# The last block's product with W34 goes between the first nine products of the second mixture; token factors move to other attention slices, and those of batch 3 to GpSimd one by one

## The chip, the core and the metric

The kernel runs on one core of a Trainium2 chip, in one launch. The metric is device time in microseconds (us) of that launch; lower is better. The core has TensorE (PE, with its weight loads as PEld), VectorE (DVE), ScalarE (ACT), GpSimd (POOL) and SyncE (SP), which here only issues DMAs. Each engine takes its instructions in the order in which the program has them, and an instruction that waits holds up those behind it.

## The reference

Three layers follow each other, all in float32: a linear attention with a decaying state, a gated product with two more matrices behind it, and eight experts whose outputs are summed with weights from a Sinkhorn iteration.

```python
# attention, batch 4, 8 heads, 768 steps, head size 48
for t in range(S):
    cur = np.einsum('bhd,bhe->bhde', u[None] * kt, vt)
    y[:, :, t] = np.einsum('bhd,bhde->bhe', rt, state + cur)
    state = wt[:, :, :, None] * state + np.einsum('bhd,bhe->bhde', kt, vt)
# first mixture, 3072 tokens, 384 -> 1024 -> 384
h = (x @ w1) * (x @ w2) @ w3
x2 = h @ w_out
# second mixture, 8 experts, 384 -> 1024 -> 384
logits = x2 @ w_gate;  P = np.exp(logits - logits.max())
for _ in range(8):
    P /= P.sum(1, keepdims=True) + 1e-09
    P /= P.sum(0, keepdims=True) + 1e-09
    P *= N / E
for e in range(E):
    out += P[:, e:e + 1] * (np.maximum(x2 @ w1[e], 0.0) @ w2[e])
```

## The kernel before

Every float32 product is made of three passes on TensorE: both operands are split into a high and a low part, and high·high, high·low and low·high are added in PSUM. ACT makes the high part (a copy that rounds), DVE or POOL the low part (a subtraction).

**First half of the program.** A loop over *slices* `s` carries the attention and the first mixture side by side. Attention has 24 units of 128 steps (6 for each of the 4 batches); a unit takes four slices: in the first, `stage_a0` starts the factors of the next unit; in the second, `stage_b` issues the score products `sc` and the transposes `trn`, and DVE masks the scores (`copy_predicated`, L329); in the third, `stage_c1` uses them (`yt<-ec,nat_v`, `up`) and DVE updates the state (`Sn`); in the fourth, `stage_c2` finishes `yt` and ACT copies it to `xraw`. The factors of the next unit are queued in `aux` and taken two for each slice; on DVE these are the two scans `Ft` and `Gt` in the first slice, `Kt` in the second, `Rt` in the third, the reduction `cc` in the fourth.

The first mixture works on blocks of 384 tokens (8 blocks, two for a batch). Each block has 8 slices `moe_a`/`moe_b` (products `pa`, `pb`, their elementwise product `gs`, its parts `gh` and `gl`), and then 4 slices `moe_x2` (18 matmuls `po` each) that multiply by W34 = w3·w_out, which was made early. ACT copies `po` into `x2[batch]`, nine slots of 128x256 for each batch. The dictionary `slices` says which slice does what. Block 7, the last, has its `moe_a`/`moe_b` in slices 99 to 106 and its `moe_x2` in 107 to 110, behind the end of attention (slice 95).

**Second half.** The second mixture multiplies tokens by the experts' w1 with a scheme that needs 15 block products instead of 18: `ORDER` is their order, `WA` and `XC` say which sums of weight blocks and of token blocks are the two factors of each. The token factors of a batch (15, each a high and a low part of 128x256) are made once, stored in DRAM (`xd`), and loaded again for each of the 16 pairs of weight rows. They come in four groups of four, four, four and three. The work is a loop over *phases* `n` = 0 to 63 (batch `n % 4`); a phase issues 15 products `zp` of six matmuls (128x256 moving), and behind each the function `after(r)` runs: it loads or makes what is due, and it takes `YN[r]` units of `y`, the second product of the phase before (24 units of three matmuls `yp`, 128x384 moving). `later(d, f)` puts a function `d` products later. Results of `zp` go through ACT copies (`cp`, L877) and DVE additions (L870, L873) into `ct`, then ACT makes `hh` (L862) and DVE `hl` (L867). Several products add on top of a bank that has to be read first: product 9 follows product 8 in bank b, with a copy on ACT between them.

**Who makes token factors.** `pre_x` makes one factor in a slice of the first half: sums on DVE (L707) at the end of a slice, the high part on ACT (L711) at the end of the next, the low part on DVE (L714) and the store to `xd` (L717) at the end of the one behind it. `PRE` gives one factor to each slice from the slice behind a batch's last `moe_x2`, for batches 0 and 1 all fifteen, for batch 2 the first eight. Scratch is `x2[3]`, the tile of batch 3, which is empty until block 6 writes it. The rest, groups 2 and 3 of batch 2 and all of batch 3, is made in phases 1 and 2 on POOL by `sp_x`, a group at a time, three products between its sums and its high part.

Of the kernel before, what the change touches and what calls it, by code (L numbers as in the profile page):

```python
# [32 lines left out]
def tile_rwkv_moe_sinkhorn_moe(  # L33
# [278 lines left out]
    def stage_b(n):  # L312
        d = st[n]
        Rt, Kt = d["R"], d["K"]
        sc = [ps.tile([P, NP, DP], F32, tag=f"sc{h}", name=f"sc{h}") for h in range(2)]
# [6 lines left out]
        pn = ps.tile([P, NP, P], F32, tag="yt0", name="trn")  # L322
# [11 lines left out]
    def stage_c1(n):  # L334
# [3 lines left out]
        up = [ps.tile([P, NP, DP], F32, tag=f"sc{c}", name=f"up{c}") for c in range(2)]  # L338
        yp = [ps.tile([P, NP, DP], F32, tag=f"yt{c}", name=f"yt{c}") for c in range(2)]
# [306 lines left out]
    def sp_w1(i, g, eng, tmp_=None):  # L646
# [91 lines left out]
    for blk in range(NB):  # L738
# [3 lines left out]
        for q in range(X2S):  # L742
# [4 lines left out]
    late = [logs.pop(x) for x in sorted(logs) if x >= NSL]  # L747
    stage_a0(0)
# [446 lines left out]
```

## Time and profile before

| | |
|---|---|
| median of 3 runs | 2028.53 us (2026.86 to 2029.04) |
| the profiled execution | 2026.48 us, of which the span from first to last instruction is 2024.7 us |
| PE busy | 1947.3 us, 96% of the span |
| DVE, ACT, POOL busy | 1429.1, 680.8, 676.7 us |
| mean granted TensorE clock | 0.99 of full speed |

The span is that of the profile and holds idle time at its start and end as well; the time of a run is a little longer than its span. A busy engine is one that has an instruction under way. In rows of the timeline, the bracket at the end is the idle time of that engine just before, and the instruction that ended it as far as the trace shows; "issue" means that it shows none.

### The profile page before, as it was taken

Reading aid. Unit: us, or ns where it says so; the run is one execution under the profiler, and the core shown is the slowest. Engines: PE = TensorE matmul, PEld = TensorE weight load, DVE = VectorE, ACT = ScalarE, POOL = GpSimd, SP = SyncE. Lnnn points to the kernel's source line nnn. Section 1 sums busy time; section 2 is a strip of 40 time slices with the busy share of each in tenths; the row PEclk is TensorE's granted clock in tenths of the full one; section 3 lists DMA queues with packets and bytes.
Section 4 is the critical chain, followed back from the end, with each engine's and each line's share of the span. In section 5 each row is a group of like instructions: output and inputs, shape, how many; then the busy total and the mean of one; then the engine's idle time right before and its main releaser. Section 6 shows DMA issues by size and latency. Waiting matters only on the chain.

```text
span 2024.7 us, 37936 instructions
## 1 busy us (share of the span) xinstructions
PE 1947.3 (96%) x15499; PEld 1882.2 (93%) x15499; DVE 1429.1 (71%) x2285; ACT 680.8 (34%) x1292; POOL 676.7 (33%) x865
## 2 busy tenths in 40 slices
PE   5779999999899999999999999999999999999999
PEld 3469898999789999999999999999999999999999
DVE  7865787864788777777666777666776666776666
ACT  4533333333333323323333333323333333333221
POOL 4676565652473122222223131322222232313200
PEclk9889999999999999999999999999999999999999
DMA  7632343423455555555455555555455555555453
GB/s 259 228 106 92 120 137 121 137 67 136 146 201 175 174 189 186 198 181 194 170 201 169 195 186 195 182 188 194 174 200 180 182 182 195 172 198 180 163 202 120
DMA packets 86125, 347.99 MB, mean 172 GB/s; under 512 B 10112, under 2 KB 30144, under 8 KB 60352
## 3 DMA queue, kind: packets, MB, share of 16 engines
q1 hardware_dynamic: 85952, 345.57, 49.5%
q8 instruction: 122, 2.00, 0.4%
q14 instruction: 51, 0.42, 0.1%
HBM read 323.90 MB, written 20.45 MB: 170 GB/s over the span
## 4 chain that ended last, share of the span: by engine, by line
PE 88%; DVE 6%; issue 2%; DMA 2%; ACT 1%; POOL 1%; SPq 1%; DVEq 0%; ACTq 0%; POOLq 0%
PE yp L85 38%; PE zp L85 33%; PE pa L85 5%; PE pb L85 5%; PE po L85 4%; DVE ct L870 1%; PE yt L85 1%; DVE hl L867 1%; PE sc L85 1%; PE trn L85 1%; PE w34ps L85 1%; PE up L85 0%; DMA nat_w<-in_w_dram 0%; DMA raw<-in_moe_w_out_dram 0%; PE pl L85 0%
## 5 line engine op out<-in xcount | busy, mean ns | idle before, releaser
L85 PE MATMUL zp<-xc,w1c 128*128 128x256 f32 x5760 | 844.4, 283 | 16.3 <-ACT ct L877 12.2
L85 PEld LDWEIGHTS zp<-xc,w1c 128*128 128x128 f32 x5760 | 792.6, 189 | 33.7 <-ACT ct L877 14.6
L85 PE MATMUL yp<-w2h,hh 128*128 128x384 f32 x1536 | 517.9, 337 | 0.0
L85 PE MATMUL yp<-w2h,hl 128*128 128x384 f32 x1536 | 517.2, 337 | 0.0
L85 PE MATMUL yp<-w2l,hh 128*128 128x384 f32 x1536 | 516.2, 336 | 0.0
L862 ACT ACTIVATE hh<-ct 128x512 fp32r<-128x512 f32 x384 | 237.7, 632 | 610.6 <-DVE ct L873 331.0
L870 DVE TENSOR_TENSOR ct<-ct,zp 128x512 f32<-128x512 f32 x576 | 381.7, 683 | 55.3 <-PE zp L85 52.8
L626 POOL TENSOR_TENSOR w1c<-w1s,w1c 128x512 fp32r<-128x512 f32 (+1 forms) x120 | 132.9, 1107 | 778.3 <-PE zp L85 477.5
L867 DVE SCALAR_TENSOR_TENSOR hl<-ct,hh 128x512 fp32r<-128x512 f32 x384 | 292.5, 775 | 0.0
L85 PEld LDWEIGHTS yp<-w2h,hh 128*128 128x128 f32 x1536 | 291.6, 190 | 0.4 <-issue 0.4
L85 PEld LDWEIGHTS yp<-w2l,hh 128*128 128x128 f32 x1536 | 288.9, 188 | 0.2 <-DVE w2l L674 0.2
L85 PEld LDWEIGHTS yp<-w2h,hl 128*128 128x128 f32 x1536 | 288.7, 188 | 0.0
L877 ACT ACTIVATE ct<-zp 128x512 f32<-128x512 f32 x256 | 152.7, 596 | 398.4 <-PE zp L85 398.4
L1027 DVE SCALAR_TENSOR_TENSOR acc<-yp,Pm,acc 128x384 f32<-128x384 f32 x336 | 205.2, 611 | 58.6 <-PE yp L85 58.5
L873 DVE TENSOR_TENSOR ct<-ct,zp 128x512 f32<-128x512 f32 x128 | 87.9, 687 | 170.7 <-PE zp L85 170.6
L873 DVE TENSOR_TENSOR ct<-zp,ct 128x512 f32<-128x512 f32 x128 | 88.5, 692 | 137.0 <-PE zp L85 133.3
L618 POOL TENSOR_TENSOR w1s<-w1raw 128x128 f32<-128x128 f32 x240 | 124.0, 537 | 9.3
L441 POOL TENSOR_TENSOR gl<-gs,gh 128x384 fp32r<-128x384 f32 x64 | 76.0, 1188 | 134.0 <-ACT gh L440 128.3
L626 POOL TENSOR_TENSOR w1c<-w1raw,w1c 128x128 fp32r<-128x128 f32 (+1 forms) x90 | 50.4, 560 | 207.8 <-ACT w1c L622 207.8
L85 PE MATMUL pa<-xhl,w1h 128*128 128x384 f32 x384 | 106.8, 359 | 2.7 <-ACT xhl L407 1.9
L85 PE MATMUL pb<-xhl,w2h 128*128 128x384 f32 x384 | 98.7, 338 | 1.6 <-ACT w2h L203 1.6
L439 DVE TENSOR_TENSOR gs<-pb,asb 128x384 f32<-128x384 f32 x64 | 35.3, 552 | 79.6 <-PE pb L85 56.2
(136 smaller groups left out, 1976.8 us busy)
## 6 DMA issues: line engine op xcount, KB each, us to landing
xc<-xd SPq DMA_DIRECT2D x188, 1024.0 KB, 4.9
xc<-xd SPq DMA_DIRECT2D x62, 768.0 KB, 4.3
w1raw<-in_e_w_dram SPq DMA_DIRECT2D x32, 384.0 KB, 3.2
w2raw<-in_e_w_dram SPq DMA_DIRECT2D x32, 384.0 KB, 3.2
xd<-x2s SPq DMA_DIRECT2D x38, 256.0 KB, 2.7
raw<-in_moe_w_dram SPq DMA_DIRECT2D x8, 1024.0 KB, 4.9
nat_w<-in_w_dram SPq DMA_DIRECT2D x24, 264.5 KB, 3.2
nat_k<-in_kt_dram SPq DMA_DIRECT2D x24, 256.0 KB, 3.9
```

Of the source, the lines that this page charges most:

```text
L85: nc.tensor.matmul(o, lhsT, rhs, start=start, stop=stop, **kw)
L439: nc.vector.tensor_tensor(gs, pb, asb, op=ALU.mult)
L441: nc.gpsimd.tensor_tensor(gl[:, f, :], gs, gh[:, f, :].bitcast(F32), op=ALU.subtract)
L618: eng.tensor_tensor(tmp_[:, many.index(r), :], at_(a), at_(b), op=ALU.add if sg == 1 else ALU.subtract)
L626: eng.tensor_tensor(lo[:, d0:d1, :], sv, hi[:, d0:d1, :].bitcast(F32), op=ALU.subtract)
L862: nc.scalar.activation(hh, src, AF.Relu)
L867: nc.vector.scalar_tensor_tensor(hl, src, 0.0, hh.bitcast(F32), op0=ALU.max, op1=ALU.subtract)
L870: nc.vector.tensor_tensor(o, a, b_, op=ALU.add)
L873: nc.vector.tensor_tensor(o, a, b_, op=ALU.subtract)
L877: nc.scalar.activation(t, src, AF.Copy)
L1027: nc.vector.scalar_tensor_tensor(dst, yp, Pm[:, tt, e:e + 1], dst, op0=ALU.mult, op1=ALU.add)
```

## The change

- `moe_x2` of block 7 leaves its four slices. Its 72 matmuls go in nine parts of eight into `after(r)` of the first nine products of phase 0. The PSUM banks of the attention get a pool of their own (`psa`), which is closed at slice 95, so that the banks `zp` (pool `psz`) exist before the first mixture is over; the banks `y`, the tiles behind `m2` and the tiles `ct` (now in pool `m`) are arranged to fit (`open2` runs behind the ninth product).
- The first eight units of `y` of phase 0 run at the end of phase 0 (two, two and four of them), the other sixteen in phase 1, one behind most products.
- `pre_x` is placed by `PLACES` and `LASTPLACES`: sums at the end of third and fourth slices of a unit, the high part in the middle of the next slice, the low part at the end of the third slice of the next unit (when the sums were in a third slice: at the end of the fourth slice of the same unit). There are four workspaces in place of three.
- Groups 2 and 3 of batch 2 are made by `pre_group` on DVE in slices 96 to 98. All of batch 3 is made by `pre_x` on POOL, one factor at a time, from product 11 on (counted from the start of phase 0; `XAT`), with four products between sums and high part.
- The weight factors of pair 1's first row (`sp_w1(2)`) go from phase 0 to phase 2, still on POOL, with a lag of five products in place of two.

```diff
+    st_pa = ExitStack()
+    psa = st_pa.enter_context(tc.tile_pool(name="psa", bufs=1, space=PSUM, side="right"))
...
+    def moe_x2(blk, i, parts=X2S):
         gh, gl = g_t[blk]
-        for m in range(i * X2N, (i + 1) * X2N):
+        n_ = KD * NF * 3 // parts
+        for m in range(i * n_, (i + 1) * n_):
...
+            tmp_ = pools["m"].tile([P, 4, P], F32, tag="w1s", bufs=2, name="w1s")
+        t = pools["m2" if k == 2 else "w"].tile([P, 2, n_, P], F32R, tag=f"w1c{k}{g}", name=f"w1c{k}{g}")
...
+    def pre_x(sb, r, work, ws, eng):
+        g = GOF[r]
+        h_ = work[:, 2 * ws:2 * ws + 2, :]
+        hr = h_.bitcast(F32R)
+        ts = sorted(terms(XC[r]), key=lambda t: t[0] == "-")
+        at_ = [x2[sb][:, SLOT[b], :] for _, b in ts]
+        sv = at_[0] if len(ts) == 1 else h_[:, 1, :]
+
+        def sums():
+            for m, (sg, _) in enumerate(ts[1:], 1):
+                eng.tensor_tensor(h_[:, 1, :], at_[0] if m == 1 else h_[:, 1, :], at_[m],
+                                  op=ALU.add if sg == "+" else ALU.subtract)
+
+        def high():
+            nc.scalar.activation(hr[:, 0, :], sv, AF.Copy)
+
+        def low():
+            eng.tensor_tensor(hr[:, 1, :], sv, h_[:, 0, :], op=ALU.subtract)
+            if (sb, g) not in xd:
+                xd[sb, g] = dram.tile([P, 2, len(XP_[g][4]), T], F32, name=f"xd{sb}{g}")
+            nc.sync.dma_start(xd[sb, g][:, :, XP_[g][4][r], :], h_)
+
+        return sums, high, low
...
+    def pre_group(sb, g, tag, tmp_, eng):
+        t = pools["w"].tile([P, 2, len(XP_[g][4]), T], F32R, tag=tag, name="xpre")
...
-    PRE = {}
-    for sb_ in range(NS - 1):
-        s0_ = 8 * UB * (sb_ + 1) + LAG + NF + X2S
-        for m_, r_ in enumerate(ORDER):
-            if s0_ + m_ < 4 * NU - 1:
-                PRE[s0_ + m_] = (sb_, r_, (m_ + 1) % 3)
-    PRED = {(sb_, g_) for sb_ in range(NS) for g_ in range(NGR)
-            if len(WP_[g_][4]) == sum(x[0] == sb_ and GOF[x[1]] == g_ for x in PRE.values())}
...
-        for q in range(X2S):
+        for q in range(X2S if blk < NB - 1 else 0):
...
+    def place(s, task, high, low):
+        event(s, lambda: task[0]())
+        event(high, lambda: task[1]())
+        event(low, lambda: task[2]())
...
+    PLACES = [4 * UB + 1 + d for d in (3, 3, 6, 7, 7, 10, 11, 11, 14, 15, 15, 18, 19, 19, 22)]
+    LASTPLACES = [4 * UB + 1 + d for d in (3, 3, 4, 6, 7, 7, 8, 10)]
+    for sb_ in range(NS - 1):
+        ends = 8 * UB * (sb_ + 1) + LAG + NF + X2S - 4 * UB - 4
+        for m_, (r_, d_) in enumerate(zip(ORDER, LASTPLACES if sb_ == NS - 2 else PLACES)):
+            s_ = ends + d_ - 0
+            low_ = s_ + {3: 3, 2: 1, 0: 2}[s_ % 4]
+            place(s_ + 0.75, lazy(lambda sb_=sb_, r_=r_, m_=m_: pre_x(sb_, r_, x2[NS - 1], m_ % 4, nc.vector)),
+                  s_ + 1.25, low_ + 0.5)
+    for g_ in range(2):
+        place(4 * NU + g_ + 0.75,
+              lazy(lambda g_=g_: pre_group(NS - 2, 2 + g_, f"xc{g_}",
+                                           pools["w"].tile([P, 4, T], F32, tag=f"w1c{g_}0", name="xtmp"), nc.vector)),
+              4 * NU + g_ + 1.25, 4 * NU + g_ + 1.5)
+    for g_ in range(2 * NGR):
+        place(4 * NU + UB + g_ + 0.75,
+              lazy(lambda g_=g_: sp_w1(g_ // NGR, g_ % NGR, nc.vector,
+                                       tx0[0][:, 2 * (g_ % 3):2 * (g_ % 3) + 2, :]
+                                       .rearrange("p a (b c) -> p (a b) c", c=P))),
+              4 * NU + UB + g_ + 1.25, 4 * NU + UB + g_ + 1.5)
+    tx0 = []
...
-        for task in fx:
-            task.pop(0)()
-        while fx and not fx[0]:
-            fx.popleft()
-        if s in PRE:
-            fx.append(list(pre_x(*PRE[s])))
-            fx[-1].pop(0)()
-        if s == 4 * NU + 1:
+            st_pa.close()
+            pools["z"] = ctx.enter_context(tc.tile_pool(name="psz", bufs=1, space=PSUM, side="right",
+                                                        reuse_waits="tile"))
...
+    PO = 9
+    YN1 = dict(zip(ORDER, (1, 1, 1, 1, 1, 1, 1, 1, 1, 1, 2, 1, 1, 1, 99)))
...
+            if n == 0:
+                i_ = ORDER.index(r)
+                if i_ < PO:
+                    moe_x2(NB - 1, i_, PO)
+                if i_ == PO - 1:
+                    open2()
+                if i_ == 11:
+                    y_fill(0)
+                y_units((0, 0, 2, 2, 4)[max(0, i_ - 10)])
+            elif n == 1:
+                y_units(YN1[r])
...
-        if n + 1 < NS and (n + 1, g) not in PRED:
-            spread(0, XLAG, sp_x(n + 1, g, nc.gpsimd))
-        else:
-            ld_x(n + 1, g)
+        ld_x(n + 1, g)
...
+    XAT = (11, 13, 14, 16, 18, 19, 21, 23, 24, 26, 28, 29, 31, 33, 34)
...
+        if n > 1:
             y_fill(n - 1)
         if n < N:
             if n == 0:
-                for i in range(2):
-                    later(8 + 3 * i, lambda i=i: sp_w2(i))
-                for g in range(NGR):
-                    later(3 * g + 1, lambda i=2, g=g: spread(0, 2, sp_w1(i, g, nc.gpsimd)))
+                for m, at_ in enumerate(sorted(ev)):
+                    later(m, *ev[at_])
+                later(8, lambda: sp_w2(0))
+                later(10, lambda: sp_w2(1))
+                for m, r in enumerate(ORDER):
+                    task = lazy(lambda r=r, m=m: pre_x(NS - 1, r, x2[2], m % 4, nc.gpsimd))
+                    d = XAT[m]
+                    later(d, task[0])
+                    later(d + 4, task[1], task[2])
             if 2 * NS <= n < 3 * NS:
                 ex.extend([lambda sb=sb, t=t: rescale(sb, t) for t in range(S // P)])
+            if n == 2:
+                for g in range(NGR):
+                    later(3 * g + 6, lambda g=g: spread(0, 5, sp_w1(2, g, nc.gpsimd)))
```

The order of instructions shows the moves at three places. First TensorE, where block 7's last product `pb` ends; `po` is the product with W34, `zp` the second mixture. Before:

```order
L85 MATMUL pb<-xhl,w2h 128x384 x2
L85 MATMUL pb<-xhl,w2l 128x384
L85 MATMUL po<-gh,w34h 128x384
L85 MATMUL po<-gl,w34h 128x384
L85 MATMUL po<-gh,w34l 128x384
```

With the change:

```order
L85 MATMUL pb<-xhl,w2h 128x384 x2
L85 MATMUL pb<-xhl,w2l 128x384
L85 MATMUL zp<-xc_5692,w1c_5643 128x256 x3
L85 MATMUL zp<-xc_5692,w1c_5797 128x256 x3
L85 MATMUL po<-gh,w34h 128x384
L85 MATMUL po<-gl,w34h 128x384
L85 MATMUL po<-gh,w34l 128x384
```

The first product of the mixture now stands ahead of the 72 matmuls `po`, eight of which follow it; the same alternation goes on up to the ninth product.

Second DVE, in the first two slices of unit 11 (batch 0's factors are being made: rows named `x2s`). Before:

```order
L270 SCALAR_TENSOR_TENSOR Ft<-nat_w_102,d_63 128x528
L439 TENSOR_TENSOR gs<-pb,asb 128x384
L273 SCALAR_TENSOR_TENSOR Gt<-nat_w_102,d_63 128x527
L714 TENSOR_TENSOR x2s<-x2s 128x256
L707 TENSOR_TENSOR x2s<-x2s 128x256 x2
L329 COPY_PREDICATED ec<-mask,sc_2540 128x256
L329 COPY_PREDICATED ec<-mask,sc_2541 128x256
```

With the change:

```order
L272 SCALAR_TENSOR_TENSOR Ft<-nat_w_105,d_63 128x528
L441 TENSOR_TENSOR gs<-pb,asb 128x384
L275 SCALAR_TENSOR_TENSOR Gt<-nat_w_105,d_63 128x527
L331 COPY_PREDICATED ec<-mask,sc_2539 128x256
L331 COPY_PREDICATED ec<-mask,sc_2540 128x256
```

Three operations of token factors no longer stand between the scans and the masking. Where they stand instead is seen best at the end of unit 13, ahead of the scans that are issued in unit 14. Before:

```order
L304 TENSOR_REDUCE cc<-rk 128x8
L714 TENSOR_TENSOR x2s<-x2s 128x256
L270 SCALAR_TENSOR_TENSOR Ft<-nat_w_103,d_63 128x528
L439 TENSOR_TENSOR gs<-pb,asb 128x384
L273 SCALAR_TENSOR_TENSOR Gt<-nat_w_103,d_63 128x527
```

With the change:

```order
L306 TENSOR_REDUCE cc<-rk 128x8
L702 TENSOR_TENSOR x2s<-x2s 128x256
L695 TENSOR_TENSOR x2s<-x2s 128x256 x4
L272 SCALAR_TENSOR_TENSOR Ft<-nat_w_106,d_63 128x528
L441 TENSOR_TENSOR gs<-pb,asb 128x384
L275 SCALAR_TENSOR_TENSOR Gt<-nat_w_106,d_63 128x527
```

One operation of token factors stood ahead of the scan there; now there are five.

Third DVE between the end of attention and block 7's first product, where the low parts `xhl` of block 7's three pieces are made. Before:

```order
L714 TENSOR_TENSOR x2s<-x2s 128x256 x2
L408 TENSOR_TENSOR xhl<-xraw,xhl 128x3x128
L714 TENSOR_TENSOR x2s<-x2s 128x256
L408 TENSOR_TENSOR xhl<-xraw,xhl 128x3x128 x2
L439 TENSOR_TENSOR gs<-pb,asb 128x384
```

With the change, from the second of the three pieces:

```order
L410 TENSOR_TENSOR xhl<-xraw,xhl 128x3x128
L628 TENSOR_TENSOR xpre<-x2s,xpre 128x256
L628 TENSOR_TENSOR xpre<-xtmp,xpre 128x768
L620 TENSOR_TENSOR xtmp<-x2s 128x256
L620 TENSOR_TENSOR xtmp<-xtmp,x2s 128x256
L620 TENSOR_TENSOR xtmp<-x2s 128x256
L620 TENSOR_TENSOR xtmp<-xtmp,x2s 128x256
L620 TENSOR_TENSOR xtmp<-x2s 128x256
L620 TENSOR_TENSOR xtmp<-xtmp,x2s 128x256
L410 TENSOR_TENSOR xhl<-xraw,xhl 128x3x128
L628 TENSOR_TENSOR xpre<-xtmp,xpre 128x768
```

Two low parts of group 2 and six sums of group 3 now stand between the second piece and the third.

## Rows read from the trace of the kernel before

**Rows 1.** The page: busy us (share of the span), instructions of TensorE.

```profile
PE 1947.3 (96%) x15499; PEld 1882.2 (93%) x15499; DVE 1429.1 (71%) x2285; ACT 680.8 (34%) x1292; POOL 676.7 (33%) x865
```

**Rows 2.** Windows: block 7's last product, then phases 0, 1, 2, 3, 4–6, 7.

```profile
core 0: us, PE busy (x) PEld busy (x) DVE busy (x) ACT busy (x) POOL busy (x), PEclk, DMA share, GB/s
490.72:503.20 12.48, 12.48 (x74) 12.48 (x74) 4.26 (x8) 2.75 (x9) 3.37 (x5) 1.00 0.59 236
503.20:519.90 16.70, 12.27 (x91) 11.05 (x91) 8.51 (x13) 7.58 (x16) 8.98 (x13) 1.00 0.54 188
519.90:550.40 30.50, 26.98 (x187) 25.66 (x186) 21.15 (x39) 8.66 (x16) 7.11 (x8) 0.94 0.40 135
550.40:576.90 26.50, 24.43 (x167) 23.52 (x166) 23.99 (x39) 10.35 (x18) 20.88 (x19) 1.00 0.40 151
576.90:605.40 28.50, 25.27 (x169) 24.90 (x168) 25.07 (x44) 9.20 (x16) 20.28 (x27) 0.94 0.54 202
605.40:680.00 74.60, 71.57 (x496) 69.99 (x495) 59.41 (x118) 24.39 (x46) 17.09 (x28) 1.00 0.53 180
680.00:703.20 23.20, 23.20 (x163) 22.99 (x162) 15.56 (x26) 7.17 (x14) 6.61 (x10) 1.00 0.50 171
```

**Rows 3.** Timeline of TensorE in phase 7: start, us, what, count.

```profile
700.25 0.87 PE L85 MATMUL zp<-xc,w1c 128*128 128x256 f32 x6
700.96 0.34 PE L85 MATMUL yp<-w2h,hh 128*128 128x384 f32 x1
```

**Rows 4.** Timeline of TensorE, waits in phases 0, 1 and 3.

```profile
517.68 3.14 PE L85 MATMUL zp<-xc,w1c 128*128 128x256 f32 x24 [1.35 <-DVE ct L870]
...
525.56 0.98 PE L85 MATMUL zp<-xc,w1c 128*128 128x256 f32 x6 [3.52 <-ACT ct L877]
...
582.08 1.65 PE L85 MATMUL zp<-xc,w1c 128*128 128x256 f32 x6 [3.23 <-ACT ct L877]
```

**Rows 5.** Windows of four attention units: 8, 11, 13 and 7.

```profile
186.83:202.67 15.84, 15.84 (x205) 14.89 (x204) 9.71 (x17) 4.74 (x11) 11.82 (x13) 1.00 0.10 28
235.24:255.24 20.00, 17.74 (x206) 16.66 (x205) 17.07 (x25) 6.16 (x16) 12.24 (x12) 0.91 0.23 75
271.85:289.81 17.96, 16.26 (x208) 15.22 (x205) 15.46 (x28) 6.50 (x15) 10.91 (x12) 1.00 0.38 123
...
170.89:186.83 15.94, 15.94 (x208) 15.03 (x205) 8.77 (x18) 5.68 (x12) 10.52 (x11) 1.00 0.27 93
```

**Rows 6.** Timeline, all engines, unit 11: masking and what stands ahead of it.

```profile
237.75 1.84 POOL L267 TENSOR_TENSOR rk<-rk,ub 128x384 f32<-128x384 f32 x1
...
238.70 1.17 DVE L714 TENSOR_TENSOR x2s<-x2s 128x256 fp32r<-128x256 f32 x1
...
239.79 1.67 DVE L707 TENSOR_TENSOR x2s<-x2s 128x256 f32<-128x256 f32 x2
...
241.38 0.77 DVE L329 COPY_PREDICATED ec<-mask,sc 128x256 f32<-128x256 uint32 x2
...
241.91 0.91 PE L85 MATMUL yt<-ec,nat_v 64*64 64x64 f32 x30 [2.26 <-issue]
...
243.28 0.42 DVE L714 TENSOR_TENSOR x2s<-x2s 128x256 fp32r<-128x256 f32 x1
```

**Rows 7.** Timelines of DVE and TensorE, unit 14: scan, masking, product.

```profile
288.63 2.07 DVE L270 TENSOR_TENSOR_SCAN Ft<-nat_w,d 128x528 f32<-128x528 f32 x1
...
292.58 0.76 DVE L329 COPY_PREDICATED ec<-mask,sc 128x256 f32<-128x256 uint32 x2
...
294.16 0.69 PE L85 MATMUL yt<-ec,nat_v 64*64 64x64 f32 x32
```

**Rows 8.** Timelines ahead of block 7: SP's stores, ACT, TensorE.

```profile
457.35 1.26 SPq L717 DMA_DIRECT2D xd<-x2s  x2
...
462.20 0.55 ACT L470 ACTIVATE x2s<-po 128x256 f32<-128x256 f32 x2 [8.68 <-DMA xd<-x2s]
...
464.66 0.44 PE L85 MATMUL pa<-xhl,w1h 128*128 128x384 f32 x1 [0.15 <-DVE xhl L408]
```

**Rows 9.** Groups by line and shape, POOL, 500 to 620 us: busy, mean ns.

```profile
L618 POOL TENSOR_TENSOR tx<-x2s 128x256 f32<-128x256 f32 x15 | 12.5, 844 | 0.4
```

More of the change, by code (lines that the diff above doesn't have):

```diff
@@ L314, in stage_b @@
         Rt, Kt = d["R"], d["K"]
-        sc = [ps.tile([P, NP, DP], F32, tag=f"sc{h}", name=f"sc{h}") for h in range(2)]
+        sc = [psa.tile([P, NP, DP], F32, tag=f"sc{h}", name=f"sc{h}") for h in range(2)]
         for p in range(NP):
@@ L321, in stage_b @@
                        True, True, pos=(64 * h, 64 * c))
-        pn = ps.tile([P, NP, P], F32, tag="yt0", name="trn")
+        pn = psa.tile([P, NP, P], F32, tag="yt0", name="trn")
         for p in range(NP):
@@ L337, in stage_c1 @@
         first = n % UPB == 0
-        up = [ps.tile([P, NP, DP], F32, tag=f"sc{c}", name=f"up{c}") for c in range(2)]
-        yp = [ps.tile([P, NP, DP], F32, tag=f"yt{c}", name=f"yt{c}") for c in range(2)]
+        up = [psa.tile([P, NP, DP], F32, tag=f"sc{c}", name=f"up{c}") for c in range(2)]
+        yp = [psa.tile([P, NP, DP], F32, tag=f"yt{c}", name=f"yt{c}") for c in range(2)]
         d["yp"] = yp
@@ L747, in tile_rwkv_moe_sinkhorn_moe, with event, run, lazy @@
     late = [logs.pop(x) for x in sorted(logs) if x >= NSL]
+    ev = {}
+    def event(at_, f):
+        ev.setdefault(at_, []).append(f)
+    def run(at_):
+        for f in ev.pop(at_, ()):
+            f()
+    def place(s, task, high, low):
+        event(s, lambda: task[0]())
+        event(high, lambda: task[1]())
+        event(low, lambda: task[2]())
+    def lazy(make):
+        box = []
+        def step(i):
+            if not box:
+                box.append(make())
+            box[0][i]()
+        return [lambda i=i: step(i) for i in range(3)]
+    PLACES = [4 * UB + 1 + d for d in (3, 3, 6, 7, 7, 10, 11, 11, 14, 15, 15, 18, 19, 19, 22)]
[19 more added lines that the diff above has]
+    tx0 = []
     stage_a0(0)
@@ L794, in tile_rwkv_moe_sinkhorn_moe @@
                 x2[si] = xp.tile([P, KD * NR, T], F32, tag="xa", bufs=NS, name="x2s")
+        run(s + 0.5)
+        run(s + 0.75)
         if s == 4 * NU - 1:
@@ L842, in z_new @@
     def z_new():
-        return ps2.tile([P, 2, T], F32, tag="z", bufs=4, name="zp")
+        return pools["z"].tile([P, 2, T], F32, tag="z", bufs=4, name="zp")
     def z_prod(bank, n, r, start, stop):
@@ L1008, in unit @@
             if first:
-                yt[b_, h_] = ps2.tile([P, DM], F32, tag="y", bufs=3, name="yp")
+                yt[b_, h_] = pools["y"].tile([P, DM], F32, tag="y", bufs=3, name="yp")
             yp = yt[b_, h_]
@@ L1068, in sk_max2 @@
-        mm(pm, ones[0:1, :], mrow[0:1, 0:1], True, True)
-        nc.vector.tensor_copy(nmx, pm)
-        nc.scalar.activation(Pm.rearrange("p t e -> p (t e)"), L.rearrange("p t e -> p (t e)"), AF.Exp,
-                             bias=nmx, scale=1.0)
+        pm = pools["y"].tile([P, 1], F32, tag="col", name="pmb")
+        mm(pm, so["ones"][0:1, :], so["mrow"][0:1, 0:1], True, True)
+        nc.vector.tensor_copy(so["nmx"], pm)
+        nc.scalar.activation(so["Pm"].rearrange("p t e -> p (t e)"), L.rearrange("p t e -> p (t e)"), AF.Exp,
+                             bias=so["nmx"], scale=1.0)
@@ L1080, in sk_rows2 @@
[L1080 removed]
+        nc.vector.tensor_tensor(so["Pm"], so["Pm"], so["rs"].unsqueeze(2).to_broadcast([P, NTT, E]), op=ALU.mult)
+        nc.vector.tensor_reduce(so["cs"], so["Pm"].rearrange("p t e -> p e t"), axis=AX.X, op=ALU.add)
     def sk_cols():
[L1083 to L1086 removed]
@@ L1087, in sk_cols @@
-        nc.vector.tensor_scalar(cs, cs, float(NT) / float(E), None, op0=ALU.mult)
+        pc = pools["y"].tile([P, E], F32, tag="col", name="pcs")
+        mm(pc, so["ones"], so["cs"], True, True)
+        nc.vector.tensor_scalar(so["cs"], pc, 1e-9, None, op0=ALU.add)
+        nc.vector.reciprocal(so["cs"], so["cs"])
+        nc.vector.tensor_scalar(so["cs"], so["cs"], float(NT) / float(E), None, op0=ALU.mult)
     def sk_cols2():
-        nc.vector.tensor_tensor(Pm, Pm, cs.unsqueeze(1).to_broadcast([P, NTT, E]), op=ALU.mult)
+        nc.vector.tensor_tensor(so["Pm"], so["Pm"], so["cs"].unsqueeze(1).to_broadcast([P, NTT, E]), op=ALU.mult)
```

113 lines of the change are left out of this document (36 added, 77 removed).

## Prediction

> **What bounds the kernel now.** The page comes first: TensorE is busy for 96% of the span [rows 1], and the change neither adds nor removes a matmul, so it can only win or lose idle time of TensorE, or clock. The windows by stage say where such time is. A phase of the second mixture that nothing disturbs is phase 7: 23.20 us for 15 products and 24 units, TensorE busy throughout [rows 2]. A product's start lies 0.71 us ahead of the next instruction's [rows 3], so 15 cost 10.7 us, and a unit costs (23.20 − 10.7)/24 = 0.52 us. The 72 matmuls of block 7's last product took 12.48 us, TensorE busy throughout, or 1.39 us for eight [rows 2]. Against these prices the start of the mixture is slow: phase 0, which has no units, took 16.70 us for 10.7 us of products; phases 1, 2 and 3 took 30.50, 26.50 and 28.50, and phases 4 to 6 together 74.60 in place of 69.6 [rows 2]. That is 6.0 + 7.3 + 3.3 + 5.3 + 5.0 = 26.9 us above phase 7's pace. The waits name the cause: in phase 0 additions on DVE, in phases 1 and 3 the ACT copy `ct` [rows 4].
>
> The windows of the attention units show a second loss. Unit 11 took 20.00 us where unit 8, its like, took 15.84; unit 13 took 17.96 where unit 7 took 15.94 [rows 5]. Units 17 and 19 repeat 11 and 13 in batch 1, so four units lose 2 × (4.16 + 2.02) = 12.4 us. The timeline of unit 11 shows how: three operations of token factors keep DVE from 238.70 to 241.4, the masking comes behind them and TensorE's `yt<-ec,nat_v` stands for 2.26 us [rows 6]. The bracket says "issue", yet the masking ends as the product starts. The rest of the 4.16 us is clock: the window's mean is 0.91 [rows 5], so 9% of 20 us, 1.8 us, is lost to a stretch at 1.2 GHz behind the gap; unit 13, with the smaller loss, shows 1.00.
>
> **Attention part.** The sums, highs and lows are the same operations at other places. In units 11, 13, 17 and 19 nothing of them is left between scans and masking, so 12.4 us can come back. They now stand in third and fourth slices, mostly where DVE is idle, but in unit 13 five of them stand ahead of the scan where one stood. An operation costs 0.42 us undisturbed and 0.84 to 1.17 with POOL at work [rows 6]. The scan of unit 14 began at 288.63; masking ended at 293.34 and the product started at 294.16, so 0.82 us are to spare [rows 7]. Four more operations cost 1.7 to 3.4 us, of which 0.9 to 2.6 us reach TensorE; I take 1.7, nearer the disturbed price, since POOL works in that slice. Batch 1 repeats it: 3.4 us. Unit 11 keeps two operations ahead of its scan as before and gives back nothing more. Net 12.4 − 3.4 = **9.0 us**. Bounds: 12.4 if the five fit, and 12.4 − 5.2 − 2 × 1.8 (two spells of half clock) − 1.4 (a store that is not through when its workspace is written again, 0.7 us twice) = 2.2.
>
> **Ahead of block 7.** Now ACT stands for 8.68 us until a store issued at 457.35 has landed and released `x2[3]`; it goes on at 462.20, 4.85 us after the issue, and the second matmul of `pa`, the first to need DVE's `xhl`, starts at 464.66 [rows 8]. With the change the last store of token factors still stands behind six small DMAs and I leave its landing between 459.7 and 461.9. Behind it come, in order, an ACT copy and the highs of group 2 (1.5 us), two lows on DVE (four times 256 columns, 1.7 us at 0.42), six sums (2.5 to 3 us) and only then the third `xhl` (0.6 us): 6.3 to 6.8 us, so 466.0 to 468.7, a loss of 1.3 to 4.0 us against 464.66. I take **2.4 us**; bounds 0, if the store lands earlier than I think, and 5.8, with 1.8 us of clock.
>
> **Start of the mixture.** Phase 0 now holds block 7's product and eight units. Its first nine products cost 9 × (0.71 + 1.39) = 18.9 us; the 1.39 us of `po` behind each cover the ACT copies that products 2 and 3 wait for. The last six cost 6 × 0.71 + 8 × 0.52 = 8.4 us, and keep the wait for DVE of 1.35 us [rows 4], as nothing stands behind products 10 to 12: 28.6 us. Phase 1 has 16 units, 19.0 us for TensorE alone. DVE's load decides there: it was busy 59.41 us in phases 4 to 6, 19.8 a phase, and 24 to 25 where POOL worked for 20 us [rows 2]. Batch 3's factors are 15 sums and 15 lows; at 0.844 us [rows 9] they are 25 us on POOL, spread over 28 products, some 13 us of it in phase 1. DVE then needs about 22.5 us (two accumulations less), and with 1.5 us of its backlog from phase 0 I take 24.0. Phases 2 and 3 share the rest with `sp_w1(2)` and `sp_w1(3)`; no group of six or more POOL operations now stands ahead of an ACT copy, and I take 25.0 each, with phases 4 to 6 at 74.0. Sum 28.6 + 24.0 + 25.0 + 25.0 + 74.0 = 176.6, against 12.48 + 16.70 + 30.50 + 26.50 + 28.50 + 74.60 = 189.3: **12.7 us** less. Bounds: at TensorE's pace in all phases (27.3 + 20.5 + 23.2 + 23.2 + 72 = 166.2) 23; with phases 1 to 6 as long as now, less 4.2 us of moved units, 4.8.
>
> On POOL and DVE the Trainium skill (page "SBUF — State Buffer", section "Who interferes with whom") speaks against the change: a DVE instruction with two SBUF inputs waits out a POOL instruction that reads SBUF, rather than sharing with it. The low part that took 1.17 us while POOL's 1.84 us operation ran, and 0.42 without it [rows 6], agrees in direction. By that rule all six `hl` of phase 1, which read `ct` and `hh`, could each wait out one POOL operation, which is the first rival below.
>
> Moved at no cost: the loads of groups 2 and 3 of batch 0 still leave when the last `pb` is through, and have eight products and 64 `po`, 17 us, to land; without that cover phase 0 would stand for what is missing. `memset` of the `ones` tile stands behind the last `po` on DVE, with DVE idle there.
>
> **Sum.** 9.0 − 2.4 + 12.7 = 19.3 us. The profiled execution took 2026.48 us, so 2007.2; the median lies 2.05 us above it, so **2009.2** on its scale. 0.2%, 4 us, is about what a measurement tells from no change.
>
> **Rivals.**
> 1. *DVE stays the bound while POOL works.* Single operations block DVE as often as groups did, and phases 1 to 6 keep their lengths: 9.0 − 2.4 + 4.8 = 11.4 us, **2017**. For it: DVE's 24 to 25 us in phases 2 and 3. Against: DVE had less to do in phase 1 and TensorE still waited, for ACT.
> 2. *All cover holds.* The five operations fit and the mixture runs at TensorE's pace: 28 to 35 us, **1994 to 2000**. Against: DVE's 19.8 us in the least disturbed phases.
> 3. *The stalls only move.* Attention gains 2.2, block 7 loses 5.8, the mixture gains 4.8: 1.2 us, **2027**, the change not doing what it says.
> 4. *Slower: ACT hangs on POOL.* Each of the fifteen highs stands on ACT, ahead of the copies `ct` that TensorE needs, and waits for POOL's sums. If each cost the 3.23 us that the group in phase 3 cost [rows 4], 48 us would be lost and the time be **2057**. It decides from 19.3/15 = 1.3 us a factor. Against: four products, some 5 us, lie between sums and high, for at most two sums of 0.84 us.
>
> **How the numbers follow.** Forecast, 2002 to 2015: 0.66. Rival 1, 2015 to 2022: 0.15. Rival 2: 0.10. Rival 3: 0.04. Rival 4: 0.05. A range from 2000 to 2019 leaves out rivals 3 and 4, half of rival 2 and an edge of rival 1. Faster takes the forecast and rivals 1 and 2: 0.91; same, rival 3: 0.04; slower, rival 4: 0.05.
>
> **What would show it.** In the profile after, units 11, 13, 17 and 19 take about 16 us and units 14 and 20 some 17.5; the first matmuls of block 7's `pa` wait 2 to 5 us; phase 0 takes 28 to 29 us with no wait in its first nine products, phase 1 about 24, with DVE busy for over 90% of it. The forecast is wrong if units 14 and 20 stand longer than 3 us, if a load of token factors ends a wait of TensorE in phase 0 or 3, or if ACT's copies in phases 1 and 2 stand behind highs that wait for POOL.

## The result and the profile after

The changed kernel takes 2007.18 us (median of 5 runs, 2005.56 to 2009.96), the kernel before 2028.53 us in the same session (5 runs, 2026.33 to 2031.01): a ratio of 0.9896, 95% interval 0.9882 to 0.9911, or 21.4 us less. The forecast was 2009.2 us and a gain of 19.3.

The profiled execution of the changed kernel is the slowest of its five (2009.96 us, span 2008.0), that of before was among the quickest of its own, so the two traces show 16.5 us of the 21.4 (16.7 in their spans). Term by term, from the traces:

| stage | before | after | gain | forecast |
|---|---|---|---|---|
| to the start of unit 6 | 154.3 | 154.3 | 0 | 0 |
| units 11, 13, 17, 19 | 75.91 | 63.56 | 12.4 | 12.4 |
| units 14 and 20 | 31.68 | 37.66 | −6.0 | −3.4 |
| unit 23 and block 7 to the end of `pb` | 49.48 | 50.42 | −0.9 | −2.4 |
| from there to phase 7 | 189.3 | 181.4 | 7.8 | 12.7 |
| phase 7 to the end | 1344.7 | 1341.3 | 3.4 | 0 |

The page of the changed kernel, engine row; TensorE has the same instructions and is busy 7.4 us less [rows 1].

```profile
PE 1939.9 (97%) x15499; PEld 1875.6 (93%) x15499; DVE 1416.7 (71%) x2299; ACT 683.8 (34%) x1300; POOL 656.7 (33%) x859
```

Windows of the changed kernel, columns as in [rows 2]: units 11, 14 and 20; then unit 23 with block 7 up to the end of `pb`; phases 0, 1, 2, 3, and 4 to 6; phases 8 to the end.

```profile
235.24:251.09 15.85, 15.85 (x207) 14.90 (x206) 14.31 (x22) 5.58 (x15) 11.87 (x12) 1.00 0.30 94
283.63:303.20 19.57, 17.68 (x205) 16.54 (x204) 15.64 (x25) 5.76 (x14) 10.89 (x12) 0.91 0.24 76
384.16:402.25 18.09, 16.19 (x205) 15.11 (x204) 15.81 (x25) 5.76 (x14) 10.90 (x12) 1.00 0.26 87
434.82:485.24 50.42, 48.38 (x405) 46.88 (x404) 32.44 (x74) 21.91 (x52) 11.61 (x11) 1.00 0.38 131
485.24:514.50 29.26, 28.17 (x188) 27.48 (x187) 15.25 (x27) 10.35 (x22) 1.84 (x2) 1.00 0.63 235
514.50:536.77 22.27, 21.60 (x161) 20.13 (x161) 14.15 (x30) 7.72 (x18) 6.82 (x10) 1.00 0.66 202
536.77:562.55 25.78, 24.25 (x167) 23.55 (x167) 21.51 (x40) 10.25 (x20) 18.69 (x25) 1.00 0.77 249
562.55:592.72 30.17, 26.17 (x168) 25.79 (x167) 23.87 (x46) 9.06 (x20) 17.95 (x29) 0.89 0.57 203
592.72:666.67 73.95, 71.17 (x495) 69.60 (x495) 59.24 (x117) 24.22 (x46) 17.09 (x28) 1.00 0.53 182
689.80:2008.01 1318.21, 1314.66 (x9145) 1300.82 (x9144) 920.61 (x1460) 419.03 (x774) 311.37 (x499) 1.00 0.52 184
```

The two of these windows that have no row ahead of the prediction, in the kernel before:

```profile
441.24:490.72 49.48, 48.59 (x405) 46.84 (x405) 26.25 (x59) 18.57 (x47) 11.22 (x11) 1.00 0.31 102
703.24:2024.72 1321.48, 1318.11 (x9145) 1304.82 (x9144) 923.40 (x1460) 419.08 (x773) 312.44 (x499) 1.00 0.53 183
```

Three places of the changed kernel fall short of the forecast or differ from it. First unit 14, timeline of DVE, POOL, ACT and TensorE:

```profile
281.91 1.03 POOL L443 TENSOR_TENSOR gl<-gs,gh 128x384 fp32r<-128x384 f32 x1 [0.20 <-ACT gh L442]
281.98 4.75 DVE L695 TENSOR_TENSOR x2s<-x2s 128x256 f32<-128x256 f32 x4
...
282.90 1.24 POOL L307 TENSOR_TENSOR ec<-eye,cc 128x512 f32<-128x512 f32 x1
...
284.10 1.19 POOL L268 TENSOR_TENSOR rk<-nat_rn,nat_kn 128x384 f32<-128x384 f32 x1
...
285.37 1.08 POOL L269 TENSOR_TENSOR rk<-rk,ub 128x384 f32<-128x384 f32 x1
...
286.65 1.24 DVE L272 TENSOR_TENSOR_SCAN Ft<-nat_w,d 128x528 f32<-128x528 f32 x1
...
288.81 0.58 ACT L328 ACTIVATE kn<-trn 128x512 f32<-128x512 f32 x1
...
289.94 1.30 PE L85 MATMUL yt<-ec,nat_v 64*64 64x64 f32 x30 [1.89 <-ACT asb L428]
```

The four sums take 1.19 us each, since POOL works beside them: each ends 0.28 to 0.29 us after one of the four POOL operations (the sums at 283.23, 284.42, 285.57 and 286.73). The scan starts at 286.65, 3.0 us after the unit; in [rows 7] it started 1.2 us ahead of it (the unit began at 289.81, [rows 5]). ACT's copy `kn` stands in turn behind work that waits for DVE. TensorE stands for 1.89 us; the mean clock of 0.91 in the window above is a stretch at 1.2 GHz behind that gap, 9% of 19.57, or another 1.8 us. Unit 20 has the same gap (1.90) and, in this execution, no such stretch.

Second, ahead of block 7 (timeline, DVE and TensorE): group 2's lows and group 3's six sums, then the third `xhl`, as forecast. The six sums cost 0.4 us each here, where POOL is idle.

```profile
456.19 0.42 DVE L620 TENSOR_TENSOR xtmp<-x2s 128x256 f32<-128x256 f32 x1
...
458.57 0.55 DVE L410 TENSOR_TENSOR xhl<-xraw,xhl 128x384 fp32r<-128x384 f32 x1
...
459.18 0.44 PE L85 MATMUL pa<-xhl,w1h 128*128 128x384 f32 x1 [2.04 <-DVE xhl L410]
```

Third, the start of phase 3. TensorE stands for 4.00 us at 568.48, and this is the chain of waits that led there (start, us, what):

```profile
551.42 4.12 DMA xd<-x2s
...
555.60 0.75 POOL x2s L695
...
557.19 0.42 ACT x2s L699
557.61 0.53 ACT hh L894
...
558.17 0.69 DVE hl L899
...
560.69 0.82 DVE Pm L1126
...
564.67 1.13 DVE rs L1111
...
566.12 0.56 DVE ct L902
...
566.70 0.63 ACT hh L894
567.33 0.61 ACT w1c L624 x2
567.94 0.49 ACT ct L909
...
568.48 1.65 PE zp L85 x6
```

Read from the top: a store of a token factor has to land before POOL may use its workspace again; POOL's two sums follow; ACT's high part of that factor has been standing on ACT for them and lets the copies `hh` behind it through; DVE, which had run dry, starts a queue of 8.5 us in which steps of the Sinkhorn iteration (`Pm`, `rs`) take 2.5; only behind that queue comes the copy `ct` that product 9 needs.

### The profile page after: what moved, and what is told of

Same layout as the page of the kernel before. It is cut to its first block, busy times and chain, and to the rows that moved or that the text cites. A ratio compares the mean times of both kernels' runs of the same rounds, so it can differ in the third digit from the quotient of the medians.

```text
span 2008.0 us, 37981 instructions
## 1 busy us (share of the span) xinstructions
PE 1939.9 (97%) x15499; PEld 1875.6 (93%) x15499; DVE 1416.7 (71%) x2299; ACT 683.8 (34%) x1300; POOL 656.7 (33%) x859
## 4 chain that ended last, share of the span: by engine, by line
PE 88%; DVE 5%; DMA 2%; POOL 2%; ACT 1%; issue 1%; SPq 0%; DVEq 0%; POOLq 0%; ACTq 0%
PE yp L85 38%; PE zp L85 32%; PE pa L85 5%; PE po L85 4%; PE pb L85 4%; PE w34ps L85 1%; PE yt L85 1%; DMA xd<-x2s 1%; DVE ct L902 1%; DVE hl L899 1%; PE sc L85 1%; PE trn L85 1%; PE up L85 1%; DMA raw<-in_moe_w_dram 0%; DMA raw<-in_moe_w_out_dram 0%
```

## Experiments

Two questions were open: which edit brought what, and what made phase 3 slow. For the second there were two theories, both about the wait of 4.00 us at the start of phase 3. **Theory 1:** ACT stands for POOL, as in rival 4, but at one place. **Theory 2:** DVE is late by its own load. All edits are to the changed kernel unless said otherwise. The runs were made in several sessions; the kernel before took 2028.1 to 2029.2 us in each of them.

**Old places of the token factors.**

```diff
-            s_ = ends + d_ - 0
+            s_ = ends + 4 * UB + 4 + m_
...
-                  s_ + 1.25, low_ + 0.5)
+                  s_ + 1.75, s_ + 2.75)
```

> The changed kernel with the old timetable of token factors (one factor a slice in batches 0 to 2, sums at the end of a slice, high part a slice later, low part two slices later); all else as changed. If the attention part is worth what the traces say, units 11, 13, 17 and 19 take 20, 18, 20 and 18 us again, units 14 and 20 go back to 15.84 us, and the kernel is 6 us slower than the changed one (about 2013). The rival, that the new places only shift stores and transfers and the gain lies elsewhere: within 2 us of the changed kernel.

2022.53 us (6 runs), 15 us more than the changed kernel. Windows of units 11 and 14:

```profile
234.95:254.95 20.00, 17.74 (x205) 16.66 (x204) 17.06 (x25) 6.16 (x16) 12.23 (x12) 0.91 0.25 80
289.51:305.35 15.84, 15.84 (x205) 14.89 (x204) 10.87 (x17) 4.62 (x11) 11.90 (x12) 1.00 0.20 66
```

These units, and unit 13 with 17.95, are those of before to 0.01 us, so the places alone make the attention term. The total was missed: in this combination unit 23 and block 7 take 55.2 us in place of 50.4, with two waits of 1.9 and 2.9 us for `xhl`, as batch 2's last factors then stand in the slices where groups 2 and 3 are made on DVE. The new places of batch 2 are worth something there that the forecast had not counted.

**Product with W34 back in its own slices.**

```diff
-        for q in range(X2S if blk < NB - 1 else 0):
+        for q in range(X2S):
...
-                if i_ < PO:
-                    moe_x2(NB - 1, i_, PO)
```

> The changed kernel with block 7's product with W34 back in its own four slices; the units of y, the token factors and the weight factors stay where the change has them. If the matmuls po hide the waits of the first nine products, product and phase 0 together take 12.5 + 16.7 + 4.2 = 33.4 us in place of 29.3, 4 us more, and the kernel takes about 2011. The rival, that moving eight units out of phase 1 and making batch 3 otherwise brought the whole gain at the start of the mixture: no difference within 1 us from the first product to phase 7.

2016.79 us (4 runs). Window from the end of `pb` to phase 1:

```profile
488.98:523.39 34.41, 29.41 (x187) 27.71 (x187) 15.59 (x27) 10.57 (x22) 1.85 (x2) 1.00 0.56 204
```

34.41 in place of 29.26: the filling is worth 5.2 us, 1 more than expected, and phases 1 and 2 are unchanged (22.25 and 25.83). Waits of 0.69 to 0.85 us stand ahead of four of the first products again. The medians differ by more, 9.6 us, the spans of the two traces by 8.4: of these, 3.4 lie in unit 20 and in unit 23 with block 7, where this execution had stretches at 1.2 GHz (from 390.93 and 462.61) that the profiled one of the changed kernel had not.

**High and low parts of batch 3's last four factors three products later.**

```diff
-                    later(d + 4, task[1], task[2])
+                    later(d + (4 if m < 11 else 7), task[1], task[2])
```

> The changed kernel, with seven products in place of four between sums and high part for the last four factors of batch 3. Theory 1: the wait of 4.00 us at the start of phase 3 comes from ACT, which stood 3.03 us for POOL's last sums ahead of two copies hh; with the later highs it falls to 1.5 us or less, no spell of half clock follows, phase 3 takes 25 to 26.5 us in place of 30.2, and the kernel gains 3.5 to 5 us. Theory 2: DVE is too late by its own load (Sinkhorn steps among its additions); phase 3 changes by less than 1 us.

2005.51 us (4 runs). Windows of unit 23 with block 7, and of phase 3:

```profile
433.55:485.94 52.39, 49.94 (x404) 48.43 (x404) 32.44 (x74) 21.89 (x52) 11.61 (x11) 0.97 0.36 125
563.58:588.66 25.08, 23.94 (x168) 23.57 (x168) 21.52 (x41) 8.10 (x19) 18.50 (x29) 1.00 0.74 263
```

And the timeline, where the wait of 4.00 us was:

```profile
566.64 0.97 PE L85 MATMUL zp<-xc,w1c 128*128 128x256 f32 x6 [1.14 <-ACT ct L909]
```

Phase 3 falls from 30.17 to 25.08, as theory 1 said. ACT's waits for POOL's sums in phases 1 and 2 fall from 12.1 to 2.2 us in all. The median is only 1.7 us lower, which the intervals of the two ratios to before (0.9870 to 0.9903, and 0.9882 to 0.9911) do not tell apart, so the gain expected in the total is not shown: in this trace block 7 has a wait of 2.45 us with a spell at 1.2 GHz behind it (clock 0.97), 2 us more than in the changed kernel's own trace.

**Sinkhorn later.**

```diff
-            if sk and at["sk"] and ORDER.index(r) % 2:
+            if sk and at["sk"] and ORDER.index(r) % 4:
...
-        at["sk"] = n >= 1
+        at["sk"] = n >= 3
```

> The changed kernel, with the Sinkhorn steps from phase 3 on in place of phase 1, eleven a phase in place of seven. Theory 2 (DVE's own load): phase 2 loses its wait of 1.10 us and phase 3 its 4.00 us, to 1.5 us or less, and the two phases together take 50 to 52 us in place of 56; phases 4 to 6, with more Sinkhorn steps, may each gain up to 1 us of waits. Theory 1 (ACT behind POOL's sums): the wait at the start of phase 3 stays above 3 us.

2015.31 us (4 runs), 8 us more than the changed kernel. Of the 4.7 us between the two spans 3.1 lie in unit 20 and in unit 23 with block 7, which the edit does not touch. The waits of TensorE from block 7's last `pb` to phase 7 (total, times, longest):

```profile
PE pcs L85 <- DVE cs L1116: 4.8, 5, 1.5
PE zp L85 <- ACT ct L909: 3.8, 4, 2.2
```

Phase 2 takes 23.69, without its first wait; phase 3's wait is 2.25 us, between what the two theories said. So the Sinkhorn steps lengthen the wait; that ACT's stand makes more of it is what the run before shows (1.14 left of 4.00). Phase 3 as a whole, which now holds eleven steps, takes 30.48 us, no less than 30.17. TensorE stands for the column sums (`pcs`) five times, a wait that was not there, and phases 4 to 6 take 77.96 in place of 73.95: phases 1 to 3 win 3.0 us together and phases 4 to 6 lose 4.0.

**The changed kernel once more.**

> The changed kernel once more, unchanged, for a second profile. If the differences between its executions are spells of half clock and the start of the program, the units from 6 on, the phases and their waits repeat within 0.1 us wherever no spell begins, and only units 0 to 5, and the places with a wait of about 2 us (units 14 and 20, ahead of block 7, phase 3), differ, by 2 us or less each.

2009.19 us (4 runs; before 2029.23, ratio 0.9903, 0.9889 to 0.9916). Units 6 to 22, and phases 0 to 2 and 4 to 7, agree to 0.06 us; phase 3 takes 30.89 (a wait of 4.23), block 7 0.2 us less. Unit 0 takes 27.53 in place of 29.23; units 0 to 5 together take 139.9 to 142.7 us in the traces of this study, whatever the edit.

**Three edits.** The late highs, and:

```diff
+    SPREAD = (8, 4, 13, 10, 9, 3, 5, 2, 7, 11, 12, 1, 6, 15, 14)
...
-        for m_, (r_, d_) in enumerate(zip(ORDER, LASTPLACES if sb_ == NS - 2 else PLACES)):
+        for m_, (r_, d_) in enumerate(zip(ORDER if sb_ == NS - 2 else SPREAD, LASTPLACES if sb_ == NS - 2 else PLACES)):
...
-        place(4 * NU + g_ + 0.75,
+        place(4 * NU + 2 * g_ + 0.75,
...
-              4 * NU + g_ + 1.25, 4 * NU + g_ + 1.5)
+              4 * NU + 2 * g_ + 1.25, 4 * NU + 2 * g_ + 1.5)
```

> The changed kernel with three edits, each at its own place. Factors of batches 0 and 1 in another order, so that the four sums ahead of unit 14's scan (and unit 20's) become none: both units at 15.84 to 16.5 us in place of 19.6 and 18.1 to 19.5. Group 3 of batch 2 two slices after group 2 in place of one, so that its sums stand behind the third xhl: the wait ahead of block 7 falls from 2.0 us or more to 0.5 or less, with no spell behind it. High parts of the last four factors of batch 3 later, as in the run before: phase 3 at 25 us. Together 11 to 15 us less than the changed kernel, 1992 to 1996. The rival, that DVE is full at these places and the waits only move to units 10 to 13 and 16 to 19: less than 7 us.

1996.6 us (4 runs, 1995.66 to 1998.39), ratio to before 0.9841 (0.9828 to 0.9855), the quickest kernel here beside the next one. Windows of unit 14, of unit 23 with block 7, of phase 3:

```profile
283.78:299.62 15.84, 15.84 (x205) 14.89 (x204) 12.22 (x22) 5.05 (x12) 11.77 (x12) 1.00 0.29 94
428.99:477.41 48.42, 48.40 (x404) 46.89 (x404) 33.01 (x74) 21.92 (x52) 11.94 (x11) 1.00 0.41 137
555.01:580.23 25.22, 23.96 (x168) 23.58 (x168) 21.61 (x41) 8.22 (x19) 18.63 (x29) 1.00 0.75 264
```

The waits of units 14 and 20 and ahead of block 7 are gone, and that at the start of phase 3 is 1.26 us in place of 4.00. The stages are shorter by 3.7 and 2.25 us (units 14 and 20), 2.0 (unit 23 with block 7) and 4.95 (phase 3), 12.9 in all, as the spans say (2008.0 and 1995.1). No unit from 6 on is longer than in the changed kernel, so no wait moved there.

**Four edits: the Sinkhorn from phase 2 on**, at seven steps a phase (`at["sk"] = n >= 2`).

> The three edits and the Sinkhorn steps from phase 2 on in place of phase 1, seven a phase as before. If phase 1 and the first wait of phase 2 lose what they lost with the late start (1.2 and 1.1 us or more) and a phase without POOL at work bears seven steps: 2 to 3 us less than with three edits. The rival, that the steps cost the same wherever they stand: the same within 1 us, with phases 6 and 7 longer by what phases 1 and 2 gain.

1995.87 us (5 runs, 1995.0 to 2003.64): the same. Phase 1 gains 0.8, phases 2 and 3 lose 0.7, phase 6 gains 0.5, phase 7 loses 0.8. The rival was right about the total; of the places it named, phase 1 gained and phase 7 lost, phase 2 and phase 6 went the other way.

**Batch 3 by groups again**, on POOL in phase 2, as before the change.

```diff
+    def sp_x(sb, g, eng):
+        t = x_tile(sb, g)
...
-        ld_x(n + 1, g)
+        if n == NS - 2:
+            spread(0, 3, sp_x(n + 1, g, nc.gpsimd))
+        else:
+            ld_x(n + 1, g)
...
-                for m, r in enumerate(ORDER):
-                    task = lazy(lambda r=r, m=m: pre_x(NS - 1, r, x2[2], m % 4, nc.gpsimd))
...
```

> The changed kernel, but with batch 3's factors made on POOL by groups again (in phase 2, three products between the sums of a group and its high part, straight into the tiles that phase 3 reads, with one tile of scratch); everything else as changed. If making them one by one is worth something by itself, phases 1 to 3 together take longer than the changed kernel's 78.2 us: about 22 + 27 + 30, as phases 2 and 3 took 26.6 and 28.5 before. The rival, that one by one brought the wait of 4 us into phase 3 (POOL waits for stores of its four workspaces, ACT for POOL), so that groups without stores ahead of the sums do better: phase 3 waits 3 us or less, and the three phases take 75 to 77 us.

2009.37 us (4 runs). Windows of phases 1, 2 and 3, then ACT ahead of phase 3's wait, which is 5.13 us:

```profile
514.72:536.97 22.25, 21.59 (x162) 20.11 (x162) 14.18 (x30) 5.17 (x10) 0.00 (x0) 1.00 0.51 186
536.97:562.15 25.18, 24.06 (x168) 23.54 (x168) 21.64 (x43) 10.43 (x18) 12.53 (x16) 1.00 0.30 105
562.15:593.73 31.58, 26.45 (x167) 26.07 (x167) 21.86 (x43) 10.58 (x22) 27.78 (x39) 0.89 0.52 204
```

```profile
567.82 0.84 ACT L624 ACTIVATE xc<-tx 128x768 fp32r<-128x768 f32 x1 [2.31 <-POOL tx L620]
568.57 0.58 ACT L921 ACTIVATE ct<-zp 128x512 f32<-128x512 f32 x1
```

The three phases take 79.0 us against 78.2, and 78.9 in the second trace of the changed kernel. Neither side of the expectation is met: that making the factors one by one is worth anything by itself is not shown, and by groups a high part on ACT stands for POOL just so, 2.31 us straight ahead of the copy. And phase 1 takes 22.25 us without one POOL instruction in it.

**Three edits, with batch 3 on DVE** (`nc.vector` for `nc.gpsimd`).

> The kernel with three edits, and batch 3's factors one by one on DVE in place of POOL. If POOL's work beside DVE costs DVE more than the operations themselves (0.42 us each on DVE alone, 30 of them, 12.6 us), phases 1 and 2 stay at 22.3 and 26.1 us or get shorter, and the kernel stays at 1996 to 1997 or gains up to 2 us. The rival, that DVE has no room in phases 1 and 2 (it was busy for 14.2 and 21.5 us there): phase 2 grows by 3 us or more.

2008.73 us (4 runs), 12 us more than with POOL. Windows of phases 1 and 2:

```profile
506.61:533.93 27.32, 23.38 (x161) 21.60 (x161) 18.11 (x42) 7.76 (x17) 0.00 (x0) 0.94 0.61 191
533.93:564.56 30.63, 26.95 (x168) 26.52 (x167) 26.81 (x59) 10.20 (x20) 2.28 (x3) 0.89 0.71 228
```

At these places DVE comes too late: TensorE waits 2.97, 3.67 and 2.39 us in phases 1, 2 and 3, and the phases are 5.1, 4.6 and 2.6 us longer. Of the two engines POOL is the better one for these factors, with these places.

**The place of one weight tile.**

```diff
-        t = pools["m"].tile([P, 2, DM], F32, tag="w2raw", bufs=2, name="w2raw")
+        t = pools["m2"].tile([P, 2, DM], F32, tag="w2raw", bufs=2, name="w2raw")
...
-        t = pools["m2" if k == 2 else "w"].tile([P, 2, n_, P], F32R, tag=f"w1c{k}{g}", name=f"w1c{k}{g}")
+        t = pools["m" if k == 2 else "w"].tile([P, 2, n_, P], F32R, tag=f"w1c{k}{g}", name=f"w1c{k}{g}")
...
-        pool = pools["m" if k == 0 else "m2"]
+        pool = pools["m2"]
...
```

> The changed kernel, with the third set of weight factors (w1c with k = 2) back in the pool on the right side of SBUF, where it was before the change, and w2raw, w2h0, w2l0 and w1s on the left in its place (w2 is loaded later, so phase 0 may be some us longer). If the place of this one tile is why phases 8 to 63 take 3.3 us less with the change than before, they take 1321 us again, and the products that read this tile lose their shorter step. The rival, that the order of instructions in a phase or the lag of w1s did it: they stay at 1318.

2015.75 us (one run; phase 0 takes 33.97, since w2 comes later). Window from phase 8 to the end:

```profile
693.05:2013.83 1320.78, 1317.29 (x9145) 1304.21 (x9144) 921.96 (x1460) 419.27 (x774) 312.53 (x499) 1.00 0.53 184
```

1320.8 us, against 1318.2 with the tile on the left and 1321.5 before: most of the gain is gone. To make room the edit also puts `w2raw`, `w1s` and the first set of `w2` on the left. That the place of `w1c` counts, and not theirs, is seen in the matmuls that read it. Three matmuls `zp` in a row share a weight row. From the start of one to the next, in phases 8 to 63, those that read the third set of `w1c` take 117.5 ns on average in the changed kernel and 120.0 in this run; those of the other two sets take 120.3 and 120.1.

## Why the prediction was right, step by step

The total was right within 2 us, but not each of its terms, and that it came so close is in part luck: their errors cancel. In the two traces they sum to 16.7 us in place of 19.3 (2.6 and 4.9 too little in attention and at the start of the mixture, 1.5 and 3.4 more than forecast ahead of block 7 and from phase 7 on); the medians, of which neither trace is typical, say 21.4. At the start of the mixture the product with W34 explains 5.2 of the 7.8 us; what the eight moved units of `y` and the later `sp_w1(2)` bring was not tried by itself.

- **Units 11, 13, 17, 19: right.** 12.4 us came back, to 15.85 and 15.94.
- **Units 14 and 20: the mechanism right, the size too small.** The term "five operations ahead of the scan, 1.7 us each unit" was measured at 3.7 and 2.25. The four sums cost 4.75 us. I bounded them by 0.84 us each, although [rows 6] show 1.17 beside POOL; at that price all four are 4.7. The wait itself, 1.89, was near the 1.7; the stretch at 1.2 GHz behind it, which I had only in the bound, was the rest. The Trainium skill's rule that I had weighed (page "SBUF — State Buffer", section "Who interferes with whom": a DVE instruction with two SBUF inputs waits out a POOL instruction that reads SBUF) agrees with 1.19 us for the sums of unit 14 and 0.4 for those ahead of block 7, where POOL is idle.
- **Ahead of block 7: right in kind, 0.9 instead of 2.4 us** in this trace. The store landed early in the interval that I left for it, and six undisturbed sums cost 2.4. Where a spell of 1.2 GHz follows the wait, as in the trace with later highs, it is 2.9 us.
- **Phase 0: right.** The first nine products start without one wait, 18.98 us against 18.9; the phase took 29.26 against 28.6. Putting `po` back costs 5.2 us.
- **Phase 1: 22.27 against 24.0, and for another reason.** "DVE's load decides there" fails: DVE is busy for 14.15 us, 64%, not over 90%, and POOL for 6.8, not 13, as POOL waits for workspaces and high parts and does its work in phase 2. Without any POOL work the phase takes as long. TensorE itself sets it, busy for 21.60 us. The matmuls of the router's logits and of their maximum (`pl`, `plt`, `pmx`, `pmb`, together busy for 1.8 us) lie there too, and my 19.0 us left them out; the other 0.8 us I can't name.
- **Phase 3: the step that failed.** "No group of six or more POOL operations now stands ahead of an ACT copy, and I take 25.0 each": phase 2 took 25.78, but phase 3 30.17. One factor's high part on ACT was enough, because POOL's sums came late, and they came late because the store that frees the workspace had not landed (POOL stood for such stores for 16.9 us in five places of phases 1 and 2). Against rival 4 I had argued that four products lie between sums and high part; that counts the sums' own time, not the time until they may start. Three products more took the whole excess away. In the kernel before, too, the group's two highs were only 1.0 of the 3.23 us [rows 4] that I had put down to them: the copy `hh` ahead of them already waited for DVE, and the copy `ct` behind them started at 581.45. ACT, before:

```profile
579.87 0.63 ACT L862 ACTIVATE hh<-ct 128x512 fp32r<-128x512 f32 x1 [0.66 <-DVE ct L870]
580.41 0.40 ACT L622 ACTIVATE xc<-x2s 128x256 fp32r<-128x256 f32 x1
```

- **Phases 8 to 63: not foreseen, 3.3 us.** I had taken these phases as unchanged, and had written that the change "can only win or lose idle time of TensorE, or clock". That premise failed: the change moves the third set of weight factors to the other side of SBUF, and the matmuls that read it take less time at the full clock, with TensorE busy throughout.

Rival 1 (DVE as the bound because of POOL) has phase 1 against it. Rival 4 was real at one place and cost about 5 us there, not 3.2 a factor. One of the signs that I had named for a wrong forecast did appear: ACT's high parts in phases 1 and 2 stood 12.1 us for POOL, and what is behind them on ACT stood with them. Of the other two, no load ends a wait of TensorE in phases 0 or 3, and in unit 14 TensorE stood for 1.89 us, though the unit lost 3.7.

## What to carry to other kernels

A task in three steps on three engines has a wait at each hand-over: the time allowed between two steps has to cover what the first one waits for, a landing store included, not only what it takes. Price an operation that is moved beside another engine at the dearest row that shows it so, not at the mean. And when matmuls of one stage fill the waits of another, look next at the phase where the moved side work now ends: the kernel with side work moved at three such places is 12.6 us quicker than the changed one (1996.6 and 2009.19, in one session).

## What the runs showed of the hardware

Where a weight tile lies in SBUF changes the pace of the matmuls that read it. In the changed kernel four phases whose two weight rows use the first and second set of `w1c`, and the four behind them, which use the third and the first:

```profile
783.01:876.24 93.23, 93.23 (x650) 92.33 (x650) 64.99 (x103) 30.23 (x58) 23.62 (x38) 1.00 0.53 187
876.24:969.00 92.76, 92.76 (x649) 91.78 (x649) 64.77 (x103) 30.14 (x57) 23.64 (x38) 1.00 0.54 188
```

TensorE is busy throughout in both, at the full clock; the second is 0.5% quicker. With the third set back on the right side all such stretches of four phases from phase 12 on take 93.15 to 93.21. The gain is that of the matmuls that read the third set, 117.5 ns from one to the next against 120.0 (experiments above). Why the place matters is open: no run varied the address within a side.

A DVE operation beside POOL can end only when the POOL operation under way has ended. The four sums of unit 14 did so, each ending 0.28 to 0.29 us after one of POOL's, and so did a much smaller one: the operation on 24 elements a partition (`rs`, L1111) took 1.13 us in the chain above and ended 0.04 us after a POOL operation that had begun ahead of it (564.50 to 565.75); in phase 1, with POOL idle, it took 0.18 us. The Trainium skill (page "SBUF — State Buffer", the same section) counts this kind, a tensor-scalar operation, among those that can take the port that DVE shares with GpSimd, and the row agrees.
